# A broadcasting load of tau and fewer places per rank in a fused attention and two-layer mixture-of-experts kernel

## The chip, the cores and the metric

The kernel runs on one core of one Trainium2 chip. The metric is the device time of one execution in microseconds (us); for a kernel it is the median of several runs. A core has TensorE (PE in the rows, with its weight loads listed as PEld), VectorE (DVE), ScalarE (ACT), GpSimd (POOL) and SyncE (SP, which here issues most DMAs).

## What is computed

Causal attention with a multiplicative forget gate feeds two layers of eight experts, each token going to its best expert alone.

```python
# q, k, v: (4, 8, 576, 64); f: (4, 8, 576)
cum = np.cumsum(np.log(np.clip(f, 1e-4, 1.0)), axis=-1)
scores = q @ k.T / sqrt(64) + cum[..., :, None] - cum[..., None, :]   # causal
attn = softmax(scores) @ v              # -> x: (2304, 512)

# layer 1: 8 experts, w1 (8, 512, 1024), w2 (8, 1024, 512)
xn = x / (norm(x) + 1e-6);  en = expert_emb / (norm(expert_emb) + 1e-6)
logits = xn @ en.T / tau                # tau: one number
expert = argmax(logits);  gate = softmax(logits)[expert]
out[mask] = gate * (relu(x[mask] @ w1[e]) @ w2[e])      # for each expert e
# layer 2: the same with logits = x @ w_gate and its own w1, w2
```

## The kernel before

**Attention.** The 32 heads are done in 16 pairs. Three strings, `PRO`, `MAIN` and `EPI`, set by hand the order in which the steps of neighbouring pairs are recorded, and that is the order on each engine's queue. A step is a name with a pair: `QSa@1` is `prep_qs` (L678) of head a of pair 1, which on GpSimd splits the loaded queries into a rounded part and a remainder (L682, L683, four instructions, into the tile `qn`); `Qa@1` is `prep_q` (L690), which transposes `qn` on TensorE (L695). `T1a@0` and its like (L815) transpose attention weights. `N1@0` is `embedding_norm` (L629): the norms of the expert embeddings `en2`, their reciprocals, the reciprocal of `tt` (tau, loaded into one partition, L623), and then a GpSimd `partition_broadcast` of it into `rtau` on 128 partitions (L638). `N2@0`, `embedding_columns` (L640), multiplies the embeddings `et` by `en2` and `rtau` later on VectorE. On GpSimd's queue `N1@0` stands directly ahead of `QSa@1`. SP loads pair 0, then `emb` and tau, then the next pairs; the loads run ahead as far as their buffers are free.

**Experts.** The experts of a layer are taken in ranks: rank 0 is the leader early on (layer 1: after three of the four batches), the others follow by number of tokens. A rank has a fixed number of *places*, from `CAPS1` for layer 1 and `CAPS2` for layer 2:

```python
CAPS1 = (384, 368, 344, 312, 304, 280, 264, 256)
CAPS2 = (560, 440, 352, 304, 280, 264, 256, 256)
```

The kernel is built for these numbers: the places of a rank are gathered in tiles of 128 rows (`tiles`), transposed into columns (`xtrans`, L521), and every matmul of the rank streams all its places as columns, empty ones too. Every product is made of three matmuls (`mm3`, L1167: rounded by rounded, rounded by remainder, remainder by rounded). A rank of C places has 96 matmuls for `w1` and 96 for `w2`, all on L1171; over 512 places each is split in two (`spans`). The first 256 places of rank 0 run early through `early_mm`, and `run` does the rest, `slice(EARLY, C)`. Weights come in chunks of 512 KB (`raw`), eight per rank, four ahead, and ScalarE and VectorE split each (L483, L484). While rank r runs, the tiles of rank r-1 go out between its `w1` steps: in layer 1 through `wg` (`out_first`, eight matmuls a tile on L1211), in layer 2 through four transposes a tile (`out_second`, L1229); the tiles of rank r+1 come in between the `w2` steps. The last rank of layer 2 does its `w2` in `last_rows`, tile by tile.

Rows of layer 1's output lie in `y_dram`, three tiles of 128 rows a rank; `routing_constants_2` (L202) writes zeros into the rows that no place fills. Tokens beyond a rank's places are handled by a general loop behind `tc.If(nv1 > 0)` (L1579) and `tc.If(nv2 > 0)` (L1627), whose tests are made from the counted tokens.

Of the kernel before, what the change touches and what calls it, by code (L numbers as in the profile page):

```python
# [8 lines left out]
F32 = mybir.dt.float32  # L9
# [5 lines left out]
ALU = mybir.AluOpType  # L15
# [4 lines left out]
P = 128  # L20
NE = 8
# [3 lines left out]
NC1 = 24 + NX  # L25
Q1, Q2 = 3, 5
BIAS = 65536.0
CAPS1 = (384, 368, 344, 312, 304, 280, 264, 256)
CAPS2 = (560, 440, 352, 304, 280, 264, 256, 256)
BASE1 = (0, 3, 6, 9, 12, 15, 18, 21)  # L30
BASE2 = tuple(5 * r for r in range(8))
XW1 = 520
# [38 lines left out]
def kernel(  # L71
# [15 lines left out]
    nc = tc.nc  # L87
# [11 lines left out]
    const = ctx.enter_context(tc.tile_pool(name="const", bufs=1))  # L99
# [21 lines left out]
    logit1 = const.tile([P, T1, NE], F32, name="logit1")  # L121
    half = const.tile([P, NT], F32, name="half")
    neg1 = const.tile([P, NT], F32, name="neg1")
    rtau = const.tile([P, 1], F32, name="rtau")

    iota128 = const.tile([P, P], F32, name="iota128")
    iota8 = iota128[:, 0:NE]
# [21 lines left out]
    def late_constants():  # L149
        nc.vector.tensor_copy(identb, ident)  # L150
        nc.gpsimd.memset(maskb, 0.0)
        nc.gpsimd.affine_select(
            out=maskb, in_=maskb, compare_op=ALU.is_ge, fill=1.0e9, base=0,
            pattern=[[-1, P]], channel_multiplier=1,
        )
        nc.vector.tensor_copy(mask2[0:TL], maskb[0:TL, 0:TL])
        nc.vector.tensor_copy(mask2[TL:], maskb[TL:, TL:])

    def routing_constants_1(_):
# [24 lines left out]
        )  # L184
        for t, caps in zip(capr, (CAPS1, CAPS2)):
            for r, x in enumerate(caps):
# [4 lines left out]
        nc.gpsimd.memset(capmask, 0.0)  # L191
        for c0, n in zip(BASE1, CAPS1):
            if n < 3 * P:
# [8 lines left out]
    def routing_constants_2():  # L202
        zrow = const.tile([P, XW2], F32, name="zrow")
        nc.gpsimd.memset(zrow, 0.0)
        for c0, n in zip(BASE1, CAPS1):
            if n < 3 * P:
# [321 lines left out]
    with ExitStack() as actx:  # L528
        p3 = actx.enter_context(tc.tile_pool(name="a3", bufs=3))
        p1 = actx.enter_context(tc.tile_pool(name="a1", bufs=1))  # L530
# [88 lines left out]
        load_pair(0, running_sum)  # L619
        et = p1.tile([NE, DM], F32, name="et")  # L620
        nc.sync.dma_start(et, emb)
        tt = p1.tile([1, 1], F32, name="tt")
        nc.sync.dma_start(tt, tau)  # L623
        late_constants()


        en2 = p1.tile([NE, 1], F32, name="en2")

        def embedding_norm(_):  # L629
            nc.vector.memset(half, 0.5)  # L630
            nc.vector.memset(neg1, -1.0)
            esq = p3.tile([NE, DM], F32, tag="sp", name="esq")
            nc.scalar.activation(esq, et, AF.Square, accum_out=en2)
            nc.gpsimd.tensor_tensor(en2, en2, half[:NE, 0:1], op=ALU.pow)
            nc.gpsimd.tensor_scalar(en2, en2, 1.0e-6, None, op0=ALU.add)
            nc.gpsimd.tensor_tensor(en2, en2, neg1[:NE, 0:1], op=ALU.pow)
            nc.gpsimd.tensor_tensor(tt, tt, neg1[0:1, 0:1], op=ALU.pow)
            nc.gpsimd.partition_broadcast(rtau, tt, channels=P)  # L638

        def embedding_columns(_):  # L640
            nc.vector.tensor_scalar(et, et, en2, rtau[:NE], op0=ALU.mult, op1=ALU.mult)
            pe = ps1.tile([P, 512], F32, tag="one", name="pe")
            for g in range(2):
                ed = p3.tile([NE, 4, 2, D], F32, tag="sp", name="ed")
                for r in range(2):
                    nc.vector.tensor_copy(
                        ed[:, :, r, :], et[:, g * 4 * D : (g + 1) * 4 * D].rearrange("e (h d) -> e h d", d=D)
                    )
                for h in range(4):
                    c = (4 * g + h) * NE  # L650
                    nc.tensor.transpose(
                        pe[:, c : c + NE], ed[:, h].rearrange("e r d -> e (r d)"), ident[:NE, :NE]
                    )
            nc.vector.tensor_copy(ie[:, :, D:], pe[:, : H * NE].rearrange("p (h e) -> p h e", e=NE))
            for r in range(2):
                nc.vector.tensor_copy(
                    ie[r * D : (r + 1) * D, :, 0:D],
                    ident[r * D : (r + 1) * D, None, r * D : (r + 1) * D].to_broadcast([D, H, D]),
                )
# [324 lines left out]
        def load(j):  # L984
            load_pair(j)
            load_cum(j)

        units = {"LD": load, "N1": embedding_norm, "N2": embedding_columns, "C1": routing_constants_1, "ST": score_t, "RT": rowmax_t, "ET": expo_t, "TT": ptrans_t, "FA": batch(route_batch),
                 "FB": batch(place_batch), "FC": batch(slot_batch), "FD": batch(sum_batch),
                 "LG": lead_rows, "LX0": lead_columns(0), "LX1": lead_columns(1), "WS0": first_weights(1)}  # L990
# [484 lines left out]
    with ExitStack() as mctx:  # L1475
# [15 lines left out]
        def after1(r):  # L1491
            n, c0 = -(-CAPS1[r] // P), BASE1[r]
            cols = slice(c0, c0 + n)
            oh, pos, hots = oh2[:, cols, :], pos2[:, cols, :], []

            def hot():
                route_a(rp, logit2[:, cols, :], pad1[:, cols], oh, n)

            def slots(p=pos):
                hots[:] = place_a(rp, p, oh, tp2[:, cols], n, Q2)  # L1500

            def places():
                route_b(
                    pq, "pl", oh, pos, tot2[r - 1], n, f"b{r}", key2 if r > NE - 3 else None,
                    slots if r == NE - 1 else None, (pt, "tr") if r == NE - 1 else None,
                )
                if r < NE - 1:
                    tot2[r] = route_total(rp, oh, tot2[r - 1], n, f"b{r}")

            def leading():  # L1510
                sig, fb, tot2[r] = lead(rp, key2, tot2[r], "2")
                lead2[0] = sig, fb
                wts.known(1, lead2[0][0], [0])

            def sums():
                place_b(pq, "pl", *hots, n, Q2, acc2, r == 0, f"b{r}")

            def rows():
                L2.early_rows(lead_index("l2e", BASE1[r + 1] * P), BASE1[r + 1] * P)

            if r == NE - 1:
                return hot, places, sums
            steps = {"h": hot, "p": places, "l": leading, "s": slots, "u": sums, "r": rows, "c": early_columns_2}
            todo = {}
            for u in (LATE if r == NE - 2 else "h4 p6 s7 u10").split():
                todo.setdefault(int(u[1:]), []).append(steps[u[0]])
            return todo
# [17 lines left out]

        L1 = Layer(True, pools, wts, x_dram, CAPS1, BASE1)
        L2 = Layer(False, pools, wts, y_dram, CAPS2, BASE2)
        got = {}
# [114 lines left out]
```

## Time and profile before

| | us |
|---|---|
| median of 3 runs (848.21 to 849.84) | 848.3 |
| the profiled execution | 852.67 |
| its span, first to last instruction | 850.9 |
| TensorE busy in the span | 794.5 (93%) |
| VectorE, ScalarE, GpSimd busy | 552.2, 483.5, 244.4 |
| data moved by DMA | 131.60 MB, mean 155 GB/s |

The span divides into attention (to about 290 us), layer 1 (to about 570) and layer 2. A busy share says little by itself here, since the stages differ; what counts in a stage is which engine the others wait for. A row of the timeline gives the start, the busy time, the engine, the line of the kernel and what is written and read; in brackets stands the idle time of the engine before it and what ended that. "issue" there means that the engine waited for nothing that the profile shows. TensorE's matmuls overlap, so a matmul's own duration is longer than the time to the next.

### The profile page before, as it was taken

The numbers are of one execution on the slowest core, as the hardware profiler recorded it, in microseconds if no ns is written. First come the engines' busy times: TensorE is split into PE (matmuls) and PEld (weight loads), VectorE is DVE, ScalarE is ACT, GpSimd is POOL, SyncE is SP. The second block draws the span as 40 slices with busy tenths as digits, with TensorE's granted clock in tenths as the row PEclk, the third lists the DMA queues.
The fourth block names the chain that finished last, engine by engine and source line by source line (L and its number), as shares of the span: only waits on it lengthen the run. The fifth ranks groups of instructions, "written<-read, shape, count | busy, mean of one in ns | idle before, by whom it ended". The sixth has DMA issues, their size and how long they took to land. (4 is left out here: it accounts for less than half of the span.)

```text
span 850.9 us, 16967 instructions
## 1 busy us (share of the span) xinstructions
PE 794.5 (93%) x5910; PEld 753.7 (89%) x5910; DVE 552.2 (65%) x1528; ACT 483.5 (57%) x1115; POOL 244.4 (29%) x456
## 2 busy tenths in 40 slices
PE   5399999999999989999999999987999999999995
PEld 3389889888889889999999999887999999999993
DVE  3277887887888846667667667744555455566661
ACT  4278878878878536455565566432534445555550
POOL 4455344344325333030330331022304032022100
PEclk9599999999999989999999999979999999999998
DMA  5456765665655235554645755452535355657640
GB/s 132 112 142 195 190 161 141 152 157 143 150 173 133 79 105 154 173 176 148 200 149 172 237 166 163 153 155 91 169 100 188 119 190 160 198 183 225 199 138 15
DMA packets 201679, 131.60 MB, mean 155 GB/s; under 512 B 85277, under 2 KB 188701, under 8 KB 201585
## 3 DMA queue, kind: packets, MB, share of 16 engines
q1 hardware_dynamic: 195425, 112.47, 46.5%
q0 software_dynamic: 5632, 17.93, 6.3%
q8 instruction: 50, 0.82, 0.4%
q14 instruction: 44, 0.36, 0.1%
q10 hardware_dynamic: 528, 0.02, 0.0%
HBM read 113.15 MB, written 18.06 MB: 154 GB/s over the span
## 5 line engine op out<-in xcount | busy, mean ns | idle before, releaser
L1171 PE MATMUL ps<-hh,w 128*128 128x280 f32 (+9 forms) x1024 | 230.4, 309 | 0.0
L1171 PE MATMUL ps<-xh,w 128*128 128x256 f32 (+9 forms) x1024 | 227.3, 306 | 2.5 <-PEq L1579 2.5
L484 DVE TENSOR_TENSOR w<-raw,w 128x1024 fp32r<-128x1024 f32 x124 | 151.6, 1224 | 57.9 <-ACT w L483 56.9
L1171 PEld LDWEIGHTS ps<-xh,w 128*128 128x128 f32 x1024 | 171.6, 190 | 4.2 <-issue 3.5
L1171 PEld LDWEIGHTS ps<-hh,w 128*128 128x128 f32 x1024 | 172.1, 189 | 1.3 <-ACT hh L1188 0.2
L1171 PE MATMUL ps<-hl,w 128*128 128x280 f32 (+9 forms) x512 | 156.8, 306 | 1.4 <-DVE hl L1189 1.4
L1171 PE MATMUL ps<-xl,w 128*128 128x256 f32 (+9 forms) x512 | 154.7, 302 | 0.0
L1188 ACT ACTIVATE hh<-ps 128x256 fp32r<-128x256 f32 (+9 forms) x144 | 58.0, 410 | 149.6 <-PE ps L1171 147.1
L483 ACT ACTIVATE w<-raw 128x1024 fp32r<-128x1024 f32 x128 | 132.8, 1052 | 0.0
L1189 DVE SCALAR_TENSOR_TENSOR hl<-ps,hh 128x256 fp32r<-128x256 f32 (+9 forms) x144 | 65.0, 457 | 59.2 <-ACT hh L1188 57.5
L1171 PEld LDWEIGHTS ps<-hl,w 128*128 128x128 f32 x512 | 97.1, 190 | 3.0 <-DVE hl L1189 2.5
L1171 PEld LDWEIGHTS ps<-xl,w 128*128 128x128 f32 x512 | 97.5, 190 | 0.3
L1239 POOL DMA_INDIRECT out_dram<-y,tok x25 | 25.7, 1029 | 184.2 <-ACT y L1235 145.2
L747 DVE CUSTOM_DVE_ANT_0 sp<-pS,cum 128x512 f32<-128x512 f32 (+3 forms) x128 | 61.0, 487 | 26.6 <-PE pS L740 25.5
L822 DVE TENSOR_TENSOR ptl<-pT,pth 128x128 fp32r<-128x128 f32 (+3 forms) x128 | 59.7, 487 | 24.1 <-ACT pth L819 24.1
L758 ACT ACTIVATE pm<-sp,sm 128x512 f32<-128x512 f32 (+3 forms) x128 | 71.3, 558 | 4.4 <-DVE sm L747 3.2
L819 ACT ACTIVATE pth<-pT 128x128 fp32r<-128x128 f32 (+3 forms) x128 | 53.8, 436 | 25.0 <-PE pT L815 23.7
L815 PE MATMUL pT<-ident,pm 128*128 128x128 f32 x320 | 58.2, 283 | 2.0 <-DVE ptl L822 1.1
L857 PE MATMUL po<-pth,vv 128*128 128x128 f32 (+2 forms) x192 | 55.9, 311 | 0.0
L282 POOL TENSOR_TENSOR l_R<-l_R,tp 128x120 bf16<-128x120 bf16 (+1 forms) x12 | 7.8, 650 | 161.5 <-DVE l_R L277 125.6
L857 PE MATMUL po<-ptl,vv 128*128 128x128 f32 (+2 forms) x192 | 53.3, 312 | 0.0
L682 POOL CAST qn<-q 128x256 fp32r<-128x256 f32 (+1 forms) x62 | 19.6, 316 | 89.6 <-PE pq L695 60.1
(313 smaller groups left out, 1496.4 us busy)
## 6 DMA issues: line engine op xcount, KB each, us to landing
raw<-in_moe_w_dram SPq DMA_DIRECT2D x128, 512.0 KB
cum<-cum_dram SPq DMA_DIRECT2D x15, 576.0 KB
k<-in_k_dram SPq DMA_DIRECT2D x64, 128.0 KB
y_dram<-y SPq DMA_DIRECT2D x17, 276.5 KB
cumt<-cum_dram SPq DMA_DIRECT2D x32, 144.0 KB
q<-in_q_dram SPq DMA_DIRECT2D x32, 128.0 KB
v<-in_v_dram SPq DMA_DIRECT2D x32, 128.0 KB
x_dram<-x SPq DMA_DIRECT2D x16, 256.0 KB
```

The lines of the kernel that those rows point to most:

```text
L483: nc.scalar.activation(hi, raw, AF.Copy)
L484: eng.tensor_tensor(lo, raw, hi.bitcast(F32), op=ALU.subtract)
L747: nc.vector.tensor_tensor_reduce(out=sp[:, :w], in0=st[j, s, "S", i][:, :w], in1=cums[j][0][:, s, :w], scale=1.0, scalar=3.0e38, op0=ALU.a ...
L758: nc.scalar.activation(pm, st[j, s, "s", i][:, :w], AF.Exp, bias=sm[:, i : i + 1], scale=-1.0, accum_out=sm[:, NT + i : NT + i + 1],)
L815: nc.tensor.transpose(pT[:, c * P : (c + 1) * P], pm[:, c * P : (c + 1) * P], ident)
L819: nc.scalar.activation(pview(j, s, "pth", i, i + 1, P), st[j, s, "T", i], AF.Copy)
L822: nc.vector.tensor_tensor(pview(j, s, "ptl", i, i + 1, P), st[j, s, "T", i], pview(j, s, "pth", i, i + 1, P).bitcast(F32), op=ALU.subtract,)
L857: nc.tensor.matmul(po[:, off + a : off + b], lhsT=vv[:, i, :], rhs=t[:, i * PSTR[s] + a : i * PSTR[s] + b], start=(i == 0 and r == 0), sto ...
L1171: nc.tensor.matmul(ps[:, :n], lhsT=l, rhs=r, start=(i == 0), stop=(i == len(steps) - 1))
L1188: nc.scalar.activation(Hh[0][:, m, sl], ps, AF.Relu)
L1189: nc.vector.scalar_tensor_tensor(Hh[1][:, m, sl], ps, 0.0, Hh[0][:, m, sl].bitcast(F32), op0=ALU.max, op1=ALU.subtract)
L1239: dma = nc.gpsimd.indirect_dma_start(out=out, out_offset=bass.IndirectOffsetOnAxis(ap=tok[:n, t : t + 1], axis=0), in_=y[:n, 0:DM], in_off ...
```

## The change

Tau is loaded into eight partitions by a DMA that reads the one number eight times, its reciprocal is taken there, and `embedding_columns` uses `tt` where it used `rtau`; the `partition_broadcast` and the tile `rtau` are gone. The places per rank get other numbers: in layer 1 ranks 0, 2, 4, 5 and 6, in layer 2 ranks 1 to 5. Ranks 5 and 6 of layer 1 and ranks 4 and 5 of layer 2 go from three tiles to two.

```diff
-CAPS1 = (384, 368, 344, 312, 304, 280, 264, 256)
-CAPS2 = (560, 440, 352, 304, 280, 264, 256, 256)
+CAPS1 = (320, 368, 320, 312, 296, 256, 256, 256)
+CAPS2 = (560, 432, 272, 272, 256, 256, 256, 256)
...
-    rtau = const.tile([P, 1], F32, name="rtau")
...
-        tt = p1.tile([1, 1], F32, name="tt")
-        nc.sync.dma_start(tt, tau)
+        tt = p1.tile([NE, 1], F32, name="tt")
+        nc.sync.dma_start(tt, tau[0, :].partition_broadcast(NE))
...
-            nc.gpsimd.tensor_tensor(tt, tt, neg1[0:1, 0:1], op=ALU.pow)
-            nc.gpsimd.partition_broadcast(rtau, tt, channels=P)
+            nc.gpsimd.tensor_tensor(tt, tt, neg1[:NE, 0:1], op=ALU.pow)
...
-            nc.vector.tensor_scalar(et, et, en2, rtau[:NE], op0=ALU.mult, op1=ALU.mult)
+            nc.vector.tensor_scalar(et, et, en2, tt, op0=ALU.mult, op1=ALU.mult)
```

Lines after the removed one are numbered one or two lower in the changed kernel. GpSimd's queue at the end of `embedding_norm` and the start of `QSa@1`, in the kernel before (`en` is `en2`, `neg` the constant -1, `qn` and `vv` the split queries and values; a row "ISA" is an instruction without a plainer name):

```order
L636 TENSOR_TENSOR en_198<-en_198,neg_81 8x1
L637 TENSOR_TENSOR tt<-tt,neg_81 1x1
L638 ISA
L638 ISA rtau<-tt 128x1
L682 CAST qn_140<-q 128x4x64
L683 ISA
L683 TENSOR_TENSOR qn_140<-q,qn_140 128x4x64
L682 CAST qn_140<-q 64x64
L683 TENSOR_TENSOR qn_140<-q,qn_140 64x64
L728 CAST vv_137<-v 128x4x64
```

The same place in the changed kernel:

```order
L635 TENSOR_TENSOR en_197<-en_197,neg_81 8x1
L636 TENSOR_TENSOR tt<-tt,neg_81 8x1
L680 CAST qn_139<-q 128x4x64
L681 TENSOR_TENSOR qn_139<-q,qn_139 128x4x64
L680 CAST qn_139<-q 64x64
L681 TENSOR_TENSOR qn_139<-q,qn_139 64x64
L726 CAST vv_136<-v 128x4x64
```

The broadcast has left the queue, and with it the two nameless ISA rows, one ahead of it and one between the CAST and the TENSOR_TENSOR of the queries; nothing else here moved.

TensorE's queue in layer 1, `w2` of rank 5, where the last tile of rank 6 comes in behind the sums of the routing (`idsb`), in the kernel before:

```order
L296 LDWEIGHTS l_ol
L296 MATMUL idsb_7293<-l_R,l_ol 128x40
L521 MATMUL xt<-ident,xg 128x8 x4
L1171 MATMUL ps<-hh,w 128x280
L1171 MATMUL ps<-hl,w 128x280
L1171 MATMUL ps<-hh,w 128x280 x2
```

And in the changed kernel:

```order
L295 LDWEIGHTS l_ol
L295 MATMUL idsb_7650<-l_R,l_ol 128x40
L1169 MATMUL ps<-hh,w 128x256
L1169 MATMUL ps<-hl,w 128x256
L1169 MATMUL ps<-hh,w 128x256 x2
```

The four transposes of the 8-row tile are gone, and the matmuls behind stream 256 columns where they streamed 280.

## Rows read from the trace of the kernel before

**Rows 1.** Waits of TensorE: us in total, times, longest.

```profile
PE pq L695 <- POOL qn L683: 13.5, 1, 13.5
...
PE xt L521 <- DMA xg<-x_dram,idxl: 3.6, 1, 3.6
```

**Rows 2.** Timeline of TensorE, 19 to 34 us: start, busy, what.

```profile
19.64 0.64 PE L815 MATMUL pT<-ident,pm 128*128 128x128 f32 x2
33.79 1.33 PE L695 MATMUL pq<-ident,qn 128*128 128x128 f32 x5 [13.51 <-POOL qn L683]
```

**Rows 3.** Timeline of GpSimd, 8 to 34 us.

```profile
8.02 0.40 POOL L682 CAST qn<-q 128x256 fp32r<-128x256 f32 x1 [1.44 <-DMA q<-in_q_dram]
8.50 0.72 POOL L683 TENSOR_TENSOR qn<-q,qn 128x256 fp32r<-128x256 f32 x1
...
9.61 0.32 POOL L683 TENSOR_TENSOR qn<-q,qn 64x64 fp32r<-64x64 f32 x1
...
17.41 0.56 POOL L636 TENSOR_TENSOR en<-en,neg 8x1 f32<-8x1 f32 x1
17.95 0.54 POOL L637 TENSOR_TENSOR tt<-tt,neg 1x1 f32<-1x1 f32 x1
24.82 0.28 POOL L638 PARTITION_BROADCAST rtau<-tt  x1 [6.34 <-issue]
24.96 0.48 POOL L682 CAST qn<-q 128x256 fp32r<-128x256 f32 x1
33.02 0.71 POOL L683 TENSOR_TENSOR qn<-q,qn 128x256 fp32r<-128x256 f32 x1 [7.58 <-issue]
```

**Rows 4.** Waits of GpSimd, the other issue row with most time.

```profile
POOL xg L513 <- issue: 10.5, 37, 0.3
```

**Rows 5.** Timeline of SP's DMA issues: the load of tau.

```profile
13.63 0.24 SPq L623 DMA_DIRECT2D tt<-in_moe_tau_dram  x1
```

**Rows 6.** Stretches: length, busy PE, PEld, DVE, ACT, POOL; clock, DMA share, GB/s.

```profile
18.00:20.00 2.00, 1.56 (x5) 0.82 (x5) 1.44 (x5) 1.19 (x5) 0.48 (x1) 0.74 0.45 103
...
26.00:28.00 2.00, 0.00 (x0) 0.00 (x0) 0.00 (x0) 0.00 (x0) 0.00 (x0) 0.50 1.11 223
...
32.00:34.00 2.00, 0.21 (x1) 0.22 (x2) 0.00 (x0) 0.00 (x0) 0.90 (x2) 0.50 0.00 0
```

**Rows 7.** Stages: layer 1, 368 and 264 places; layer 2, 440, 304, 280, 264, 256.

```profile
340.30:376.80 36.50, 36.50 (x240) 36.16 (x238) 24.80 (x68) 19.02 (x38) 6.71 (x7) 1.00 0.52 159
...
504.70:533.30 28.60, 28.28 (x236) 27.32 (x235) 20.84 (x54) 16.96 (x35) 5.68 (x7) 1.00 0.62 188
...
634.35:676.15 41.80, 41.80 (x226) 39.06 (x225) 21.36 (x41) 17.40 (x30) 8.56 (x8) 1.00 0.43 138
...
710.15:739.45 29.30, 29.30 (x219) 29.07 (x218) 17.23 (x30) 15.63 (x29) 6.66 (x6) 1.00 0.57 181
739.45:766.65 27.20, 27.20 (x218) 26.99 (x217) 16.88 (x30) 15.05 (x29) 5.00 (x5) 1.00 0.64 194
766.65:792.10 25.45, 25.45 (x214) 25.39 (x213) 16.16 (x27) 14.53 (x26) 5.19 (x5) 1.00 0.69 208
792.10:816.70 24.60, 24.60 (x213) 24.51 (x212) 16.00 (x28) 14.34 (x26) 3.91 (x3) 1.00 0.65 192
```

**Rows 8.** Timeline of TensorE, rank 0 of layer 1, `w1`.

```profile
313.14 0.39 PE L1171 MATMUL ps<-xh,w 128*128 128x128 f32 x2
...
321.85 0.39 PE L1171 MATMUL ps<-xh,w 128*128 128x128 f32 x2
```

**Rows 9.** Timeline of TensorE: a full and a 24-row tile through `wg`.

```profile
344.35 1.09 PE L1211 MATMUL pr<-wg,yt 128*128 128x136 f32 x8
345.18 0.42 PE L1171 MATMUL ps<-xh,w 128*128 128x368 f32 x1
...
512.60 1.11 PE L1211 MATMUL pr<-wg,yt 128*24 128x136 f32 x8
513.63 0.40 PE L1171 MATMUL ps<-xh,w 128*128 128x264 f32 x1
```

## Prediction, made before the changed kernel was run

> **What bounds the kernel now.** The program is one long TensorE program, so I first asked who TensorE waits for. The list of its waits is short: one of 13.5 us on POOL's `qn` (L683); the next of the two quoted, a gather, is 3.6 us [rows 1]. TensorE's timeline places the first: a transpose `pT` begins at 19.64 and lasts 0.64, so TensorE is free at 20.28, and the next transposes, those of `qn` (L695), begin at 33.79 [rows 2]. POOL's timeline gives the cause. POOL ends the reciprocal of tau (L637) at 18.49; PARTITION_BROADCAST (L638) runs at 24.82 after 6.34 us of "issue" idleness; the CAST behind it runs at 24.96; the TENSOR_TENSOR of L683 runs at 33.02 after a second 7.58 us [rows 3]. Nothing released either gap. The same operation at 8.50 had no gap, and the other issue gaps quoted for POOL are at most 0.3 us each (37 of them) [rows 4]. The order of instructions has an ISA row ahead of the broadcast and another between CAST and TENSOR_TENSOR, exactly where the gaps are; both rows are gone from the changed kernel. [...]
>
> From 340 us on the reader should look at one stage per rank: TensorE is busy the whole stage (36.50 of 36.50, 24.60 of 24.60) at full clock, and the DMA engines are busy 0.43 to 0.69 of it [rows 7]. There each column less is time less, as long as a matmul's time follows its columns.
>
> **The change part by part.**
>
> *tau.* POOL loses the broadcast and both gaps. After L637 at 18.49 the four steps of `qn` need what they needed at 8.02 to 9.93 [rows 3], so the TENSOR_TENSOR that TensorE waits for ends at about 18.5+0.48+0.72 = 19.7, ahead of 20.28 when TensorE comes free. The wait of 13.5 us is gone whole: **13.5 us**. The 8x1 reciprocal in place of 1x1 costs nothing: the 8x1 one ahead of it, L636 at 17.41, took 0.56 where L637 took 0.54 [rows 3].
>
> What is late next? The pair-1 queries must be in SBUF by 18.5. They are issued right after tau, whose issue is at 13.63 and 0.24 long [rows 5]; the broadcasting form writes eight elements and may issue a few tenths later, pushing the loads queued behind it on SP by the same. If tau itself lands late, POOL's L637 waits, and the cover is 20.28-19.7 = 0.6 us; beyond that each us costs one. The loads for the next pair run ahead during the stall: 223 GB/s at 26 to 28 us, then 0 at 32 to 34 [rows 6], that is, they finished while nothing used them. In the changed kernel they run beside work. If all that landed up to 32 were needed at the restart at 20.3, 11.7 us of the 13.5 would be lost; but the queue is served in order, and pair 1's part is the earlier one, so I charge nothing, and 7 us as the bad end. [...] Bounds of this part: 6.3 (only the first gap goes) to 14.5.
>
> *Columns.* Per rank 192 matmuls of `mm3` (L1171) stream the rank's places. Stages with equal tile work give the price: 304 places 29.30 us, 280 places 27.20 [rows 7]: 2.10/24 = 0.0875 us a column and rank (0.456 ns per matmul and column). Layer 2 drops 8+80+32+24+8 = 152 columns on ranks 1 to 5: 152x0.0875 = **13.3 us**. In layer 1 the stages of 368 (36.50) and 264 (28.60) differ by 7.9 us on 104 columns [rows 7], 0.076, of which I take 0.075: ranks 2, 4, 5 and 6 drop 24+8+24+8 = 64 columns: **4.8 us** (5.6 by layer 2's price).
>
> *Rank 0 of layer 1* drops 64 as well, but its first 256 columns are done early, so in `w1` (96 matmuls) 128 columns become 64, and in `w2` (96) 384 become 320. `w2`: 96x64x0.456 ns = **2.8 us**. For `w1` the row nearest is the 128-column one: 26 groups of three between 313.14 and 321.85 [rows 8], 112 ns each, although the 256-column stage has only (24.60-5x0.35)/192 = 119 ns (0.35 for each tile's transposes, below). Halving from 256 to 128 gained 7 ns, so I take **0** for halving again; the other end is half of 112, 96x56 ns = 5.4 us. [...]
>
> *Tiles.* 280 and 264 places were three tiles of 128, 256 is two. Two ranks in each layer lose a tile. In layer 1 a 24-row tile's eight `wg` matmuls take 512.60 to 513.63, 1.03 us [rows 9]; the four transposes on the way in are worth 27.20-25.45-16x0.0875 = 0.35 (those stages differ by 16 columns and one such tile [rows 7]). Layer 1: 2x(1.03+0.35) = 2.8; layer 2, with four transposes in and four out: 2x(0.35+0.35) = 1.4. Against it, ranks 0 and 2 now end in a 64-row tile, and a short tile's `wg` block takes 1.03 where a full one takes 345.18-344.35 = 0.83 [rows 9]: 0.2 each, -0.4. Sum **3.8 us**.
>
> *Zero rows.* One more zeroing DMA and 128 more zero rows (283 KB) during attention, on SP and the queues, where DMA has room: 0, at worst 1 us.
>
> **Sum:** 13.5+13.3+4.8+2.8+3.8 = 38.2 us. The profiled execution took 852.67 (span 850.9), 4.4 above the median 848.3; 38.2 off gives 814.5 for a profiled execution and 848.3-38.2 = 810.1, so **810** for the median.
>
> **The rivals.**
>
> *Only the first gap goes.* If the second 7.58 us belongs to L683 or to something that stays, the early gain is 6.3, and the time 848.3-6.3-24.7 = 817. For it: the CAST between the two gaps ran without delay, so the two are not one. Against: L683 ran at 8.50 without a gap, and its ISA row vanishes. [...]
>
> *The weights become the bound.* A rank of 256 places needs eight chunks of 512 KB, 4.2 MB, and about 1.1 MB of rows in and out (two tiles of 128 rows of 2,212 bytes each way). At 24.6 us that is 215 GB/s; the fastest stage shown moves 208 at a DMA share of 0.69 with TensorE full [rows 7]. If 194 GB/s, what the 280-place stage moves, were the limit, each such stage would take 27.3 us, 2.7 more; over the six ranks of 256 with such traffic 16 us at most, some 8 if half of it shows: 818. Against: one stage already runs 208, and 2-us stretches run above that [rows 6].
>
> *Early loads.* The earlier start waits for the loads of pairs 1 and 2: up to 7 us of the 13.5 given back, 817.
>
> *Slower: the general path.* A rank with more tokens than places sends the rest through the loop behind `tc.If(nv1 > 0)`, which the profile of before doesn't show at all. The reference's routing on its own inputs, worked out in double precision, has 360, 313, 312, 305, 292, 250, 244, 228 tokens per expert in layer 1 and 559, 429, 269, 269, 256, 255, 136, 131 in layer 2. Rank 0 of layer 1 is the leader after three of four batches: 272 tokens against 269 for the next, and it ends with 313, under the new 320. Were the runner-up (360) to lead, 40 tokens would overflow: one tile with its 4.2 MB unprefetched at 138 to 208 GB/s [rows 7] is 20 to 30 us, the repeated routing, gathers and early matmuls of layer 2 (64+32 of 119 ns are 11 us) at least as much again, with the stops between them some 60 to 75: about 875. It decides at a three-token swing. In layer 2 an expert has exactly 256 tokens for 256 places; its nearest tie, 4e-4 of the largest logit, is wide for the hi/lo split matmuls. One overflow there adds a loop of 25 to 40 us at the end, about 840.
>
> **How the numbers follow.** The forecast (810, by itself 805 to 815) has 0.77; only the first gap 0.05; weights 0.08; early loads 0.06; general path 0.04, most of it in layer 1 and above 848. The bottom adds the upper early bound (1), layer 1's other slope (0.8) and part of the 5.4 us of the 64-column matmuls: 805. The top takes in the three rivals at 817 to 818: **805 to 818**. About 0.2% is what a measurement here can tell from no change. Faster by more than that 0.96, within it 0.01, slower 0.03.
>
> **What would show it.** Right: no wait of TensorE on `qn` above 1 us and no idle issue gap on POOL near 18 us; the transposes of `qn` at about 20.3; layer-2 stages of 26 to 27.5 us for the 272-place ranks and 24.5 to 25 for the 256-place ranks behind them; the 64-column matmuls still near 112 ns; TensorE full through the stages. Wrong: a gap of 6 or 7 us on POOL that remains; TensorE's `ps` waiting on DVE's or ACT's `w` in the 256-place stages; any row from the general loop.

## Result

The changed kernel takes 825.8 us (median of 4 runs, 824.20 to 827.05) beside 849.1 for the kernel before (4 runs on the same chip, 848.21 to 850.51): a ratio of 0.972, interval 0.970 to 0.975. The direction was forecast, the size was not: 38 us were forecast and 23 came, and 825.8 lies 7.8 us above the top of the range. Its profiled execution took 827.05, span 825.3; between the two profiled executions lie 852.67-827.05 = 25.6 us, and these are what the following accounts for.

The early part went as forecast. GpSimd's timeline and, below it, TensorE's (start, busy, what), which answer to [rows 3] and [rows 2]:

```profile
18.57 0.54 POOL L636 TENSOR_TENSOR tt<-tt,neg 8x1 f32<-8x1 f32 x1
19.07 0.39 POOL L680 CAST qn<-q 128x256 fp32r<-128x256 f32 x1
19.54 0.74 POOL L681 TENSOR_TENSOR qn<-q,qn 128x256 fp32r<-128x256 f32 x1
```

```profile
20.00 0.64 PE L813 MATMUL pT<-ident,pm 128*128 128x128 f32 x2
20.43 1.27 PE L693 MATMUL pq<-ident,qn 128*128 128x128 f32 x5
```

Both gaps are gone, and the transposes of `qn`, which began at 33.79, begin at 20.43 without a wait. The waits of TensorE (us in total, times, longest) have no row for `qn` left; the gather is there as in [rows 1], and one short wait for split weights, 1.6 us:

```profile
PE xt L520 <- DMA xg<-x_dram,idxl: 3.7, 1, 3.7
...
PE ps L1169 <- POOL w L483: 1.6, 1, 1.6
```

The stages of layer 2 came within half a microsecond of the lengths forecast. Ranks 2 to 6 (272, 272, 256, 256, 256 places), beside [rows 7] (length, busy PE, PEld, DVE, ACT, POOL; clock, DMA share, GB/s):

```profile
664.90:692.30 27.40, 27.40 (x221) 27.18 (x220) 17.66 (x31) 15.10 (x29) 6.56 (x6) 1.00 0.56 183
692.30:718.80 26.50, 26.50 (x214) 26.41 (x213) 16.53 (x27) 14.49 (x26) 4.97 (x5) 1.00 0.65 202
718.80:743.50 24.70, 24.70 (x214) 24.64 (x213) 15.80 (x27) 14.34 (x26) 5.55 (x5) 1.00 0.71 215
743.50:767.60 24.10, 24.10 (x211) 24.10 (x211) 16.18 (x28) 13.94 (x26) 4.24 (x4) 1.00 0.75 220
767.60:791.70 24.10, 24.10 (x210) 24.10 (x209) 16.15 (x28) 13.87 (x26) 2.02 (x2) 1.00 0.67 198
```

TensorE is busy the whole of each, at full clock, while up to 220 GB/s move.

What went wrong shows when the program is cut at the first matmul of each stage and the lengths are set beside each other (worked out from the two timelines; "early" are the first 256 columns of a layer's rank 0, with the wait for the gather, and "rest" means the columns behind them):

```
stage                     before   after   gain   sum of gains
up to early, layer 1      289.37  275.65   13.7   13.7
early, layer 1             21.43   21.16    0.3   14.0
rank 0 w1, rest            11.49   20.33   -8.8    5.2
rank 0 w2                  18.05   16.86    1.2    6.3
ranks 1 to 7, layer 1     232.62  225.68    6.9   13.3
early, layer 2             19.84   19.83    0.0   13.3
rank 0 w1, rest, layer 2   14.78   17.32   -2.5   10.7
rank 0 w2, layer 2         26.77   26.79    0.0   10.7
ranks 1 to 7, layer 2     205.74  191.43   14.3   25.0
```

(The sums are rounded one by one. The last stage is measured to the start of its last matmul, and the last 0.6 us lie behind it.) One stage streams half as many columns as before and takes 8.8 us longer. Three rows of TensorE's timeline in it, beside [rows 8]:

```profile
297.09 0.61 PE L1169 MATMUL ps<-xh,w 128*128 128x64 f32 x2
297.52 0.40 PE L1169 MATMUL ps<-xl,w 128*128 128x64 f32 x1
297.73 0.61 PE L1169 MATMUL ps<-xh,w 128*128 128x64 f32 x2
```

Three matmuls from 297.09 to 297.73 are 213 ns each, where 128 columns took 112. 96 of them are 20.4 us, the whole stage. The stretches of 3 us tell why (length, busy PE, clock, DMA share, GB/s); first the kernel before, where the 128-column matmuls run from about 311 to 322, then the changed one, where the 64-column matmuls run from 296.8 to 317.1:

```profile
306.00:309.00 3.00, 1.67 (x8) 0.50 0.64 180
309.00:312.00 3.00, 3.00 (x17) 0.50 0.49 150
312.00:315.00 3.00, 3.00 (x26) 0.91 0.00 0
315.00:318.00 3.00, 3.00 (x29) 1.00 0.03 5
```

```profile
291.00:294.00 3.00, 0.53 (x4) 0.83 0.64 165
294.00:297.00 3.00, 3.00 (x16) 0.50 0.70 191
...
306.00:309.00 3.00, 3.00 (x16) 0.50 0.00 0
...
315.00:318.00 3.00, 3.00 (x14) 0.50 0.00 0
318.00:321.00 3.00, 3.00 (x16) 0.62 0.55 182
321.00:324.00 3.00, 3.00 (x23) 1.00 0.81 253
```

In both, the granted clock goes down to 0.50 in the wait for the gather (before from 1.00 at 304 to 305 us to 0.50 at 306 to 307, after from 0.98 at 292 to 293 to 0.50 at 293 to 294). In the kernel before it is up again some 5 us after work resumes, less than 2 us into the 128-column matmuls. In the changed one it stays at 0.50 through the whole stretch of 64 columns and rises when `w2` streams 320.

### The profile page after: what moved, and what is told of

It reads as the page before. It is cut to its first block, busy times and chain, and to the rows that moved or that the text cites. A ratio compares the mean times of both kernels' runs of the same rounds, so it can differ in the third digit from the quotient of the medians.

```text
span 825.3 us, 16797 instructions
## 1 busy us (share of the span) xinstructions
PE 778.5 (94%) x5863; PEld 739.0 (90%) x5863; DVE 545.7 (66%) x1510; ACT 474.1 (57%) x1095; POOL 237.2 (29%) x450
## 5 line engine op out<-in xcount | busy, mean ns | idle before, releaser
L1169 PE MATMUL ps<-xh,w 128*128 128x256 f32 (+8 forms) x1024 | 226.5, 308 | 3.5 <-PEq L1577 2.2
L1169 PE MATMUL ps<-hh,w 128*128 128x256 f32 (+7 forms) x1024 | 218.8, 301 | 0.0
L1169 PEld LDWEIGHTS ps<-xh,w 128*128 128x128 f32 x1024 | 176.6, 199 | 5.0 <-issue 4.5
L1169 PEld LDWEIGHTS ps<-hh,w 128*128 128x128 f32 x1024 | 168.7, 189 | 1.1 <-ACT hh L1186 0.2
L1169 PE MATMUL ps<-xl,w 128*128 128x256 f32 (+8 forms) x512 | 155.7, 304 | 0.0
L1169 PE MATMUL ps<-hl,w 128*128 128x256 f32 (+7 forms) x512 | 153.1, 299 | 1.4 <-DVE hl L1187 1.3
L1186 ACT ACTIVATE hh<-ps 128x256 fp32r<-128x256 f32 (+8 forms) x144 | 56.1, 397 | 148.8 <-PE ps L1169 146.2
L1187 DVE SCALAR_TENSOR_TENSOR hl<-ps,hh 128x256 fp32r<-128x256 f32 (+8 forms) x144 | 62.8, 441 | 62.7 <-ACT hh L1186 61.5
L1169 PEld LDWEIGHTS ps<-xl,w 128*128 128x128 f32 x512 | 101.9, 199 | 0.2
L1237 POOL DMA_INDIRECT out_dram<-y,tok x23 | 23.1, 1005 | 175.4 <-ACT y L1233 138.7
```

What stands on the lines that cost most here:

```text
L1169: nc.tensor.matmul(ps[:, :n], lhsT=l, rhs=r, start=(i == 0), stop=(i == len(steps) - 1))
L1186: nc.scalar.activation(Hh[0][:, m, sl], ps, AF.Relu)
L1187: nc.vector.scalar_tensor_tensor(Hh[1][:, m, sl], ps, 0.0, Hh[0][:, m, sl].bitcast(F32), op0=ALU.max, op1=ALU.subtract)
L1237: dma = nc.gpsimd.indirect_dma_start(out=out, out_offset=bass.IndirectOffsetOnAxis(ap=tok[:n, t : t + 1], axis=0), in_=y[:n, 0:DM], in_off ...
```

## Experiments

Two explanations of the 213 ns stood against each other. **A, the clock:** a matmul of few columns takes 213 ns at the lower level and 112 at the higher, and a stream of such matmuls doesn't bring the clock up. **B, the matmul itself:** 64 columns are a slow shape at any clock. Each diff below is against the changed kernel unless it says otherwise, and each ratio is against runs of the kernel before on the same chip. The experiments ran on three chips, so times of different batches are compared with care, and what a stage took is read from the profiles.

### The two parts of the change apart

`tau_only` has the new load of tau and the old places; `places_only` the old tau and the new places.

```diff
# tau_only (and tau_only_2, the same kernel again)
-CAPS1 = (320, 368, 320, 312, 296, 256, 256, 256)
-CAPS2 = (560, 432, 272, 272, 256, 256, 256, 256)
+CAPS1 = (384, 368, 344, 312, 304, 280, 264, 256)
+CAPS2 = (560, 440, 352, 304, 280, 264, 256, 256)
# places_only, against the kernel before: the same lines the other way
```

> Only the tau part of the change; places as before. If the tau part is worth what the changed kernel's timeline shows at the end of attention (early layer-1 matmuls begin 13.8 us earlier), this runs 849.1-13.8 = 835.3 us, and the two gaps of GpSimd are gone. If part of that gain is given back later (loads that no longer run ahead, a stage that starts at another clock level), it runs 838 or more.

> Only the new places; tau as before, so the 13.5 us wait of TensorE is back. If the two parts simply add, 849.1-(23.3-13.8) = 839.6 us, with rank 0's rest of w1 in layer 1 (64 columns) at about 20 us, where 128 columns took 11.5. If the 64-column stretch is slow only because the tau part moved it in time, that stretch is near 11 us here and the time near 831.

Measured: `tau_only` 839.7 us (834.20, 834.65, 844.82, 847.55), ratio 0.987, interval 0.974 to 1.000. `places_only` 837.7 (834.86 to 839.88), ratio 0.984, interval 0.975 to 0.994. Two runs of `tau_only` came where they were expected and two some 10 us later; more on them below. `places_only` came within 2 us of the plain sum.

In the profile of `places_only` the stage in question takes 17.23 us, neither of the two lengths expected, and its inside decides between A and B. Its 64-column matmuls begin at 309.72. Stretches of 2 us, and two rows of the timeline:

```profile
306.00:308.00 2.00, 1.62 (x8) 0.58 0.56 146
308.00:310.00 2.00, 2.00 (x14) 0.56 0.75 193
310.00:312.00 2.00, 2.00 (x20) 1.00 0.15 60
312.00:314.00 2.00, 2.00 (x17) 0.79 0.03 8
314.00:316.00 2.00, 2.00 (x11) 0.50 0.00 0
```

```profile
309.88 0.39 PE L1171 MATMUL ps<-xh,w 128*128 128x64 f32 x2
310.21 0.39 PE L1171 MATMUL ps<-xh,w 128*128 128x64 f32 x2
```

Here the clock came up just as the narrow stream began, and three matmuls take 0.33 us (the single one between the two rows is left out): 110 ns each, what 128 columns took. So 64 columns aren't slow in themselves, and B falls. Then, at about 313, some 3.4 us into the stream, the clock goes from 1.00 to 0.50 with TensorE busy 2.00 of 2.00 us, and the rest of the stage runs at the lower level. A was too weak: in this stream the clock didn't only fail to rise, it fell. Whether the width did that, the runs below tell.

Around the wait ahead of the stage, with TensorE busy 0.00 of 2.00 us and then 1.62, the clock had gone from 1.00 (304 to 306 us) to 0.58 (306 to 308); the fall at 313, under a busy share of 2.00 of 2.00, is not told by a busy share as the profile counts it.

### Giving rank 0 its columns back

`r0_384` gives rank 0 of layer 1 its 384 places again and leaves the other fifteen numbers new. `r0_wide` keeps 320 places and only makes the stretch 128 columns wide, the last 64 of which are computed and not used; `places_wide` does the same to `places_only`.

```diff
# r0_384
-CAPS1 = (320, 368, 320, 312, 296, 256, 256, 256)
+CAPS1 = (384, 368, 320, 312, 296, 256, 256, 256)
# r0_wide, places_wide
-self.xtrans(t, self.xg[0], self.caps[0], self.x)
+self.xtrans(t, self.xg[0], max(self.caps[0], EARLY + P), self.x)
...
-self.w1_step(m, wts.ws[b + m // 2], slice(EARLY, C), X, Hh)
+self.w1_step(m, wts.ws[b + m // 2], slice(EARLY, max(C, EARLY + P)), X, Hh)
```

> The changed kernel with rank 0 of layer 1 back at 384 places, so that the rest of its w1 streams 128 columns instead of 64. Both readings of the 64-column stretch (low clock that it does not lift, or a matmul form that is slow in itself) expect that stretch back at 11.5 us from 20.3 and w2 at 18 from 16.9: 825.8-7.7 = 818 us. If the missing 12.6 us lie elsewhere, more places cost what I had priced: 825.8+2.8 = 828.6.

> The changed kernel with 320 places in rank 0, but the rest of its w1 streams 128 columns: the third tile is transposed whole, and its last 64 columns are computed and not used. More work in 96 matmuls, and nothing else. If the width of these matmuls is what cost the time, 20.3 goes to 11.5 us and w2, begun at the full clock, gains about 1 more: 816 us. If the number of places (tiles of 64 rows, their transposes and stores) is what cost it: 826 us.

> Only the new places, tau as before, and the rest of w1 of rank 0 in layer 1 on 128 columns. This is the part of the prediction on columns and tiles alone, without the narrow stretch. The terms as predicted, 13.3+4.8+2.8+3.8 = 24.7, give 849-24.7 = 824.4 us. If the columns were over-priced elsewhere too, it runs 830 or more.

Measured: `r0_384` 821.1 (814.34, 817.39, 824.77, 825.43), ratio 0.967, interval 0.957 to 0.977. `r0_wide` 814.8 (812.30, 813.20, 816.43, 823.45), ratio 0.959, interval 0.949 to 0.970. `places_wide` 828.4 (824.83 to 832.47, 6 runs), ratio 0.976, interval 0.971 to 0.980. The stage takes 11.23, 10.91 and 11.59 us in their profiles, with twice the columns of the changed kernel's 20.33. Sixty-four columns that nobody needs shorten this stage and the `w2` behind it, together, from 34.17 to 27.53 us between `places_only` and `places_wide` and from 37.19 to 26.84 between the changed kernel and `r0_wide`: 6.6 and 10.4 us. The medians differ by 9.3 (837.7 and 828.4) and 11.0 (825.8 and 814.8), but each of these pairs comes from two batches of runs, and other stages differ too. `places_wide` also missed what was expected of it, 824.4, by 4.0 us, and no run here shows where these went. Stretches of `r0_wide`:

```profile
294.00:296.00 2.00, 2.00 (x12) 0.50 0.70 164
296.00:298.00 2.00, 2.00 (x19) 0.97 0.23 92
298.00:300.00 2.00, 2.00 (x21) 1.00 0.03 8
```

The clock rises as the 128 columns begin and stays. But `r0_384` has two runs near 825, no better than the change itself, and `r0_wide` one at 823. The mean granted clock of these three is 0.967, 0.967 and 0.964, that of the shorter runs 0.979 to 0.985: something goes one of two ways.

### Is it the wait, the width, or both?

`fill_64` fills the wait for the gather with three more groups of `w1` matmuls of 256 columns, 36 in all, whose results aren't used. `fill_wide` has that and the wide stretch. `r0_352` makes the stretch 96 columns wide. `l1_old` gives all of layer 1 its old places.

```diff
# fill_64, fill_wide
-TURN1 = "... m6 e5 x2 m7 e6 e7"
+TURN1 = "... m6 e5 F x2 m7 e6 e7"
...
+def filler():                    # "F"
+    for i in range(3):
+        L1.w1_mm(6, wts.ws[3], slice(0, EARLY), x0)
# fill_wide: also the two lines of r0_wide
# r0_352
+CAPS1 = (352, 368, 320, 312, 296, 256, 256, 256)
# l1_old
+CAPS1 = (384, 368, 344, 312, 304, 280, 264, 256)
```

> The changed kernel with 36 more matmuls of 256 columns (their results are not used) where TensorE waits 3.7 us for the third tile of rank 0, so that it enters the 64-column stretch at the full clock. Theory A (the narrow stream lets the clock fall even while TensorE is never idle): the stretch begins at 112 ns a matmul and ends at 213, 15 to 18 us in place of 20.3, and the time is 821 to 824. Rival A2 (the clock is low only because of the wait ahead of it): the clock stays at 1.00, the stretch takes 10.8 us and the time is about 816. Rival B (a 64-column matmul takes 213 ns at any clock): 20.3 us, 826 or more.

> The kernel with the 128-column rest of w1 (320 places) and the 36 extra matmuls in the wait. If they keep the clock up, the last early matmuls (0.5 of the clock there) gain about 1.3 us over the same kernel without them, less what the extra matmuls overrun the wait, at most 1: 814 to 816. If they delay the third tile's transposes, 817.

> The changed kernel with 352 places in rank 0 of layer 1, so that the rest of its w1 streams 96 columns. If 96 columns still keep or raise the clock, the stretch takes 11 us as with 128 and the time is about 817; if they let it fall as 64 do, 17 to 20 us and 825 to 828.

> Tau part and the new places of layer 2; layer 1's places as before. From the stages of the changed kernel, layer 1's new places gain 7 us in ranks 1 to 7 and lose 7.7 in rank 0, and the first stage of layer 2 is 2.5 us longer with the new places at unchanged width. If that is all, this kernel is 1 to 4 us faster than the changed one: 822 to 825, with the first stage of layer 2 (304 columns) back at 14.8 us from 17.3. If the 2.5 us came with layer 2's places or with the tau part, that stage stays at 17.

Measured: `fill_64` 817.6 (812.31 to 818.02), ratio 0.961, interval 0.950 to 0.973. `fill_wide` 810.1 (809.74 to 810.59), ratio 0.955, interval 0.948 to 0.962. `r0_352` 824.8 (822.77 to 827.84), ratio 0.971, interval 0.962 to 0.980. `l1_old` 826.4 (818.92, 821.34, 831.42, 833.16), ratio 0.977, interval 0.957 to 0.996. `fill_64` and `fill_wide` came out 3 to 4 us below what was expected of them, and `l1_old`, expected at 822 to 825, with two runs below that and two above.

Stretches of `fill_64`, whose 64-column matmuls begin at 297.42:

```profile
298.00:300.00 2.00, 2.00 (x20) 1.00 0.27 96
300.00:302.00 2.00, 2.00 (x20) 1.00 0.00 0
302.00:304.00 2.00, 2.00 (x17) 0.82 0.00 0
304.00:306.00 2.00, 2.00 (x11) 0.50 0.00 0
```

Without the wait the clock is at 1.00 when the narrow stream begins and falls some 6 us into it, with no idle time in the stage; the stage takes 14.98 us, where A expected 15 to 18, while the time of 817.6 is nearer to the 816 of its rival A2. The stage decides between them: of the 9.2 us by which this profile is shorter than the changed kernel's, 5.4 are gained in the stage and 2.4 at the start of layer 2. So neither the wait nor the drop that it makes is needed for a loss. In `fill_wide`, on the same chip, with no wait and 128 columns, the clock is at 1.00 throughout, and the stage takes 10.81:

```profile
290.00:292.00 2.00, 2.00 (x20) 1.00 0.75 234
...
304.00:306.00 2.00, 2.00 (x19) 1.00 0.37 118
```

The two kernels differ in the width of this stretch alone, so it is the narrow stream that makes the loss; the stage and its `w2` take 5.8 us more in `fill_64`, and the median is 7.5 us longer. One of the four runs of `fill_64`, which has no profile, took 812.31 at a mean clock of 0.985, where the other three have 0.974 and 0.975: the loss may not come every time.

`r0_352` met its 96 columns at 0.50 and stayed there to its end, 20.35 us for the stage, the same time as with 64:

```profile
294.00:296.00 2.00, 2.00 (x12) 0.50 0.73 173
...
314.00:316.00 2.00, 2.00 (x10) 0.50 0.00 0
```

Whether the clock would fall from 1.00 in a stream of 96 columns, this run doesn't show.

### The same kernel again

`tau_only` had two times 10 to 13 us apart, and its profile was one of the shorter. `tau_only_2` is the same kernel run again, for a profile of the longer.

> Only the tau part, a second time with more rounds, since the runs of the first time scattered over 13 us. If the tau part is worth what the timelines show at the end of attention (13.8 to 16 us), 849-14 = 835 us against a before of 849, and the ratio is 0.983 with an interval clear of 1. If the scatter was the kernel's own (its stretches fall at other clock levels from run to run), it stays as wide here.

Measured: 840.4 (834.72, 836.16, 836.22, 844.53, 844.83, 848.11), ratio 0.986, interval 0.980 to 0.992; the profiled execution took 844.83. The interval is clear of 1, and the scatter is as wide as the first time. Stretches of the shorter, then of the longer:

```profile
292.00:294.00 2.00, 2.00 (x12) 0.52 0.69 183
294.00:296.00 2.00, 2.00 (x20) 1.00 0.37 119
```

```profile
292.00:294.00 2.00, 2.00 (x11) 0.50 0.71 221
294.00:296.00 2.00, 2.00 (x11) 0.50 0.51 144
...
314.00:316.00 2.00, 2.00 (x10) 0.50 0.00 0
316.00:318.00 2.00, 2.00 (x9) 0.59 0.75 248
```

One program, two levels. The stage takes 10.66 us in the one and 20.37 in the other, `w2` behind it 18.07 and 19.18; 9.7 and 1.1 us, as much as the spans differ (832.4 and 843.0). In the kernel before, `tau_only`, `r0_wide` and `fill_wide` the clock was at 1.00 within the first 2 us of the stretch of 128 columns, and none of them shows a fall in it (11.49, 10.66, 10.91 and 10.81 us for the stage; `r0_384` and `places_wide`, with 11.23 and 11.59, lie near these); in `tau_only_2` it had not come up by then and stayed down to the end. Which of the two happens differs from one execution to the next of the same program. That accounts for the two values of `tau_only`, and those of `r0_384` and `r0_wide` fit it, though no long run of these has a profile; so does `fill_wide`, which, without the wait, spreads over only 0.85 us. The kernel before has long runs too, none of them profiled: on the chip of `tau_only`, 857.20 and 858.07 at a mean clock of 0.963 and 0.965, beside five from 845.85 to 849.20 at 0.978 to 0.982. What decides it within an execution no run here shows.

### The first stage of layer 2

This stage has 304 columns in both kernels and took 2.5 us longer. Stretches of 4 us, before and after:

```profile
592.00:596.00 4.00, 3.20 (x13) 0.57 0.05 10
596.00:600.00 4.00, 4.00 (x31) 1.00 0.75 200
```

```profile
580.00:584.00 4.00, 2.71 (x11) 0.50 0.19 44
584.00:588.00 4.00, 4.00 (x22) 0.69 0.73 204
```

In both the clock is low behind two waits, one for a gather (2.5 us before, 2.7 after) and, right ahead of the stage, one on TensorE's own sequencer at the test of the general loop (2.5 before, 2.2 after), and after the change the clock comes back later in the stage. The changed kernel also has an idle gap inside the stage, which nothing in the profile released; the kernel before has none (a row of the waits and one of the timeline, both of the changed kernel):

```profile
PE ps L1169 <- PEq L1577: 2.2, 1, 2.2
...
582.27 0.67 PE L1169 MATMUL ps<-xh,w 128*128 128x304 f32 x2 [1.29 <-issue]
```

Over the profiles the stage takes 13.4 to 17.5 us: 14.8 to 15.0 in the kernel before, `tau_only`, `l1_old`, `fill_64` and `fill_wide`, 13.4 in `tau_only_2`, 17.0 to 17.5 in the changed kernel and the other five. These six are just the ones with such a gap, of 0.9 to 1.6 us and at the same place in TensorE's instructions; the other six have none. So 1.3 of the 2.5 us are the gap, and the rest is time at the lower clock. `l1_old` was to tell which part of the change brings it: with the new tau and layer 2's new places the stage is back at 14.8. `fill_64` and `fill_wide` have all the new places, so the new numbers alone don't force it either. What makes the gap, and whether the gap keeps the clock down, stays open.

## Why the prediction was wrong, step by step

**tau: right.** 13.5 forecast, 13.7 measured where layer 1 begins. That the two agree to 0.2 us is in part luck: the two kernels with tau alone began layer 1 16.1 and 15.6 us ahead of the kernel before, `fill_64` 12.4, and `places_only` and `places_wide`, without the new load, 0.7 and 1.1, so attention itself varies by some microseconds between profiles. Both idle gaps of [rows 3] went; the rival that only the first would go fell. The trace of the kernel before shows two gaps, 6.34 and 7.58 us, and nothing of what fills them. Reading the two vanished instructions off the order was the step that carried this. Early loads took nothing back either, and the zero rows cost nothing that shows: the two kernels with the new places and the old tau began layer 1 earlier than the kernel before, not later.

**Layer 2, columns and tiles: right.** 13.3 and 1.4 forecast, 14.3 measured on ranks 1 to 7. The rival of the weights fell: stages of 256 places ran at 215 and 220 GB/s with TensorE full.

**Layer 1, ranks 1 to 7: right.** 4.8 for columns and 2.4 for tiles forecast, 6.9 measured; over the profiles of kernels with these places the gain is 6.8 to 11.1, so the close agreement is in part luck here too. The general path was not entered: no row of its loop stands in the profile.

**Rank 0 of layer 1, `w1`: the step that failed.** The prediction took 0 and bounded it by a gain of 5.4; the stage lost 8.8. The failure is not the 112 ns: at the upper clock 64 columns do cost what 128 do, as `places_only` showed (110 ns). In the changed kernel all 96 matmuls ran at 0.50 and took 213 ns each. The failure is that the term was priced at the upper clock only, from [rows 8], and that the bounds were drawn as if a loss were excluded, though nothing excluded it. The rows to price it otherwise were there: the 3.6 us wait of [rows 1] ends at 307.33, 3.5 us ahead of this stage, and [rows 6] show a clock of 0.50 in the wait of 13.5 us. The first matmuls of this very stage, which [rows 8] leave out, ran at the lower level in the kernel before:

```profile
311.12 0.63 PE L1171 MATMUL ps<-xh,w 128*128 128x128 f32 x2
...
311.76 0.63 PE L1171 MATMUL ps<-xh,w 128*128 128x128 f32 x2
```

Three matmuls from 311.12 to 311.76 (the single one between the rows is left out) are 213 ns each, for 128 columns. At that price 96 matmuls lose 96x(213-112) ns = 9.7 us against [rows 8], and this is the end of the bounds that was missing. With it the range would have reached 820, still short of 825.8, mostly by the two terms below. The 0 was an estimate from the 7 ns between the 256-column and the 128-column matmuls, both at the upper clock; the trace of `places_only` agrees with it at 1.00 (110 ns) and that of the changed kernel shows 213 ns at 0.50, and I didn't ask at which level the stage would run.

**Rank 0, `w2`: mis-sized.** 2.8 forecast, 1.2 measured. At full clock all through (`fill_wide`) 320 columns take 15.92 us where 384 took 18.05, so 2.1 are the columns; 0.9 more went to the clock, which rose only some 3 us into the stage.

**The clock's allowance: too small.** The 1 us from 13.5 up to the bound of 14.5 was an allowance for the granted clock, in the early part alone, and no run shows it: the starts of layer 1 given above lie 12.4 to 16.1 us ahead of the kernel before where the new load is in. The first stage of layer 2 lost 2.5 us without an edit of its own, 1.3 to the idle gap and the rest to the clock (0.50 and 0.69 in the two stretches above, 0.57 and 1.00 before).

Added up: of the 12.6 us that are missing (38.2 against 25.6), 8.8 went in rank 0's `w1`, 1.6 in its `w2`, 2.5 at the start of layer 2; and 0.7 in ranks 1 to 7 of the two layers, against 0.5 gained in attention and the early matmuls and 0.6 behind the last stage. `fill_wide`, which takes away the loss in rank 0 and in which the start of layer 2 didn't fall back, is the fastest version here: 810.1, 15.8 us below the change (in another batch of runs; the ratios are 0.955 and 0.972). That 810.1 is also the time forecast is luck: between the two profiles it gains 42.8 us where the terms gave 38.2, among it 1.4 in the early matmuls, which had no term, and 2.0 more than forecast in ranks 1 to 7 of layer 1.

**The sign that failed.** The prediction named "the 64-column matmuls still near 112 ns" among the signs of being right. They took 213, and of its signs this is the one that pointed at the failed step.

## What to carry to other kernels

Columns taken from a stage were worth time only down to some width: here a matmul of 64 columns took 110 ns and one of 128 took 112, at the upper clock, so the last 64 columns gave nothing, and the long stretch of narrow matmuls ran at a TensorE clock of 0.50. Price every such stretch at both levels of the clock, and look for the wait just ahead of it. Padding the stretch, or filling the wait with work, may be the cheaper choice: here 64 useless columns were worth 6 to 10 us in the two stages of rank 0.

## What the runs showed of the hardware

- In an unbroken stream of 64-column matmuls, each behind its own 128-column weight load, the granted clock fell from 1.00 to 0.50 while the profile shows TensorE busy 2.00 of 2.00 us (`places_only` 3.4 us into it, `fill_64` some 6 us into it).
- Streams of 64, 96 and 128 columns were each seen at 0.50 from beginning to end, 20.33, 20.35 and 20.37 us for 96 matmuls (212 ns each whatever the width); the clock came back 2.4 to 5.6 us into the 320 to 384 columns of `w2` behind them. In the kernel before, `tau_only`, `r0_wide` and `fill_wide`, in which 128 columns ran at 1.00, it did not fall in that stretch.
- GpSimd's `partition_broadcast` had cost two idle spans, 6.34 us ahead of itself and 7.58 us ahead of the next TENSOR_TENSOR; removing the one call removed both.
